# First product of the first layer in four of six token blocks, written as seven products of sums, with another opening

## The chip, the cores and the metric

The kernel runs on one core of one Trainium2 chip. The metric is device time in microseconds (us) for one launch: the median of the runs shown. TensorE is called PE here, its weight loads PEld, VectorE DVE, ScalarE ACT, GpSimd POOL, and SP is the engine whose queue issues nearly all DMAs.

## What is computed

A linear attention with decay (4 batches, 8 heads, 768 steps, head size 64) gives 3072 tokens of 512 values. Two layers follow, each with an input product to 2048 and an output product back to 512.

```
for t in range(S):
    state = gamma * state + k[t] (outer) v[t]
    y[t] = scale * q[t] @ state
x = y as (3072, 512)
h = x @ w_in;  x = maximum(0.01 * h, h) @ w_out        # first layer
h = x @ w2_in; out = (h * cos(h)) @ w2_out             # second layer
```

## The kernel before

**Numbers.** All data are float32. For a large product each operand is split into a rounded high part and the low rest, and `mm3` (L360 to L363) issues three matmuls: high by high, low by high, high by low. Weights arrive as int64 words, and are rounded in steps: two ACT operations (`exponent`), two on DVE (`fraction`, `top_bits`), an integer addition on POOL (`round_up`, L139), an ACT cast to the high part and a DVE subtraction for the low part. The 32 half tiles of the first layer's weights (16 slices `f`, parts 0 and 1) pass through this at the start; the second layer's weights later, in the same way, with results stored to HBM (`w2d`, `w2i`).

**Blocks.** Tokens go in six blocks of 512. The attention works in 24 units of 128 steps; an `excursion` is a unit's run of 64x64 matmuls, for unit u ("here") and for the scores of unit u+1 ("ahead") together. In the first layer a block needs, for each of 16 slices `f`, `gemm1` (12 matmuls 128x512 into PSUM bank `p`), the leaky ReLU on ACT, a split into high and low (`high_g` on ACT, `low_g` on DVE), and the second product (12 matmuls 128x512 into four banks `acc`), one to three slices later. Blocks 0 and 1 are cut at slices 7 and 4 (`SPLIT`) and alternate, since their weights are still being made; blocks 2 to 5 run whole, with the attention of the block ahead and the second layer's weights beside them.

**Second layer.** It handles two blocks at a time, and its input product already goes by 2x2x2 pieces: seven products of sums in place of eight (names P1 to P7), with the weights' sums in `w2i` (1.83 MB for two slices), loaded in four DMAs, and the tokens' sums in `xq`. Its matmuls are 128x512.

**Order.** Everything stands in an order written by hand: strings (`LOADS`, `FIRST`, `SLOTS`, `TICKS`) for the opening, lists of steps by half slices afterwards, and an `Agenda` of moments (two per slice) for the second layer's weights: a half slice takes three moments, a pair of slices nine. Each engine runs its instructions in that order, and a DMA on SP waits until the eighth DMA before it has landed.

Of the kernel before, what the change touches and what calls it, by code (L numbers as in the profile page):

```python
# [24 lines left out]
P = 128  # L25
# [8 lines left out]
SPLIT = (7, 4)  # L34
# [26 lines left out]
XMADE = ("P1", "P2", "P3", "P5", "P7", "P6", "P4")  # L61

# [17 lines left out]
def body(ctx: ExitStack, tc: tile.TileContext, att, w1, w2, tab, out):  # L80
# [57 lines left out]
    def round_up(raw, t):  # L138
        nc.gpsimd.tensor_tensor(out=t, in0=t, in1=raw[:, :, 0], op=ALU.add)  # L139
# [7 lines left out]
    class Weights:  # L147
# [26 lines left out]
        def pieces(self):  # L174
# [34 lines left out]
    xq = [[dpool.tile([P, 1024], F32, name=f"xq{s}_{i}") for i in range(14)] for s in range(1, NB // 2)]  # L209
# [87 lines left out]
    def xprep(agenda, m, s, xlow=None, step=13):  # L297
# [9 lines left out]
        for k in range(2):  # L307
            way = {}
            for i, name, keep in ((0, "P1", True), (1, "P2", True), (3, "P3", True), (0, "P5", False), (2, "P7", False), (3, "P6", False), (1, "P4", False)):
                j = 7 * k + XMADE.index(name)  # L310
                if s == 0:
                    way[name] = parts(place(i), partial(own_x, j), 0, xlow or nc.vector, keep, None)
                else:
                    way[name] = parts(place(i), xq[s - 1][j], 0, nc.vector, keep, ostage, False)
# [17 lines left out]
    def load_xq(s, j):  # L332
        assert ("x", s) in made
        xt[j] = w_tile(j, 0, F32R, 1024)
        nc.sync.dma_start(out=xt[j].bitcast(F32), in_=xq[s - 1][j])

    def own_x(j):
        if j not in xt:
            xt[j] = w_tile(j, 0, F32R, 1024)
# [9 lines left out]
    wi = {}  # L349

    def load_wi(p, place):
        assert ("p", p) in made
        for old in [o for o in wi if wi[o][1] == place]:
            del wi[old]
        t = xpool.tile([P, 4096], F32R, tag=f"b{place}", name=f"b{place}")
        wi[p] = t, place
        for lo, hi in ((0, 1024), (1024, 2048), (2048, 3072), (3072, WIN)):
            nc.sync.dma_start(out=t[:, lo:hi].bitcast(F32), in_=w2i[p][:, lo:hi])
# [7 lines left out]
    class Attention:  # L366
        def __init__(self, apool, tb):
            self.apool, self.tb = apool, tb
            self.spare = [w_tile(NF - 1 - i // 2, i % 2, F32, 1024) for i in range(2 * EARLY)]
# [3 lines left out]
        def part(self, d, u, part, tag, bufs):  # L373
            if u < EARLY:
                d[u] = self.spare[2 * (EARLY - 1 - u) + part]
# [23 lines left out]
        def excursion(self, now, nxt, banks):  # L399

            sc, kv, po = (b.rearrange("p (n i) -> p n i", n=H) for b in banks)
# [58 lines left out]
        def tokens(self, u, xh, xl, tok0):  # L460
            x = self.apool.tile([P, KD, C], F32, tag="xs", name="xs", bufs=2)
# [11 lines left out]

    def new_x(n):
# [5 lines left out]
    def gemm1(key, f, x, hp):  # L480
        w = wslot[key, f, 0]
        xh, xl = x
        for k in range(KD):
# [21 lines left out]
    with tc.manual_schedule():  # L505

        with ExitStack() as pctx, ExitStack() as actx:
            apool = actx.enter_context(tc.tile_pool(name="apool", bufs=1))
            tb = apool.tile([P, NTAB], F32, name="tb", bufs=1)
            heads = Attention(apool, tb)  # L510

            NU = B * NCH
            xs = {}

            def excursion(u, banks):
                heads.excursion(u if u >= 0 else None, u + 1 if u + 1 < NU else None, banks)

            def evacuate(u):
                n = u // CPB
                if n not in xs:  # L520
# [8 lines left out]
            def unit_steps(u):  # L529
                def both():  # L530
                    excursion(u, [bank(i) for i in (1, 2, 3)])
                    scored(u + 1)
                    evacuate(u)
                    heads.lower[u](nc.gpsimd)
# [11 lines left out]
                return [both, int, state, int, values, int, int, int]  # L546

            def block_steps(n):
                return [step for u in range(n * CPB, n * CPB + CPB) for step in unit_steps(u)]

            agenda = Agenda()
            START, LAST = 4, 2 * (NF * (NB - 3) - 4)
            m, turn = 0, 0
# [10 lines left out]
            def half(f):  # L567
# [4 lines left out]
                high, low = parts(t, w2d[f], 0, nc.gpsimd, False, ostage)  # L572
# [37 lines left out]
            OWN = 4  # L610
            for p in range(OWN):
                for f in range(4 * p, 4 * p + 4):
                    half(f)
                pair(p)
            xprep(agenda, max(m + 3, LAST + 5), 0, nc.gpsimd)
# [395 lines left out]
```

## Time and profile before

| | us |
|---|---|
| median of 3 runs | 1105.61 (1105.3 to 1107.13) |
| the profiled execution | 1106.15 |
| its span, first to last instruction | 1104.4 |
| PE busy | 1078.5 (98% of the span) |
| DVE busy | 650.2 (59%) |
| ACT busy | 488.4 (44%) |
| POOL busy | 225.1 (20%) |

A busy PE is not PE at its peak: matmuls are pipelined, and a record's length is not the distance to the next one. The distance between starts is what counts. The granted clock is given as a share of 2.4 GHz; 0.50 is the lower level of 1.2 GHz.

### The profile page before, as it was taken

What the parts mean: (1) busy time and instruction counts of PE and PEld (TensorE: products, weight loads), DVE (VectorE), ACT (ScalarE), POOL (GpSimd) and SP (SyncE); (2) the same over time, 40 slices, a digit from 0 to 9 for tenths busy, and PEclk for the clock granted to TensorE, in tenths of its full rate; (3) what the DMA queues carried; (4) which work ended last, traced back from release to release, by engine and by line L of the source; (5) the groups of instructions that cost most, each with busy time, mean ns of one, the idle gap of its engine ahead of it and who ended that gap; (6) DMA issues with size and microseconds to landing.
All of it is one profiled execution on the core that took longest, in us unless ns stands there. A gap on an engine that the chain in (4) does not pass through costs nothing.

```text
span 1104.4 us, 18719 instructions
## 1 busy us (share of the span) xinstructions
PE 1078.5 (98%) x7484; PEld 893.3 (81%) x7484; DVE 650.2 (59%) x973; ACT 488.4 (44%) x842; POOL 225.1 (20%) x174
## 2 busy tenths in 40 slices
PE   4899999999999999999999999999999999999998
PEld 4678888888887887888888888888888888888887
DVE  3687843122444434333587677777767777656665
ACT  3677632223434334333554455544445544444432
POOL 3454421112434343332465000000000000000000
PEclk8799999999999999999999999999999999999999
DMA  9455422233545535533696436676446585423412
GB/s 366 165 195 203 153 77 83 72 115 115 170 151 191 177 123 189 173 108 116 196 326 240 144 135 226 211 283 229 142 173 239 183 311 207 164 72 143 156 54 77
DMA packets 71367, 189.22 MB, mean 171 GB/s; under 512 B 8048, under 2 KB 10352, under 8 KB 71280
## 3 DMA queue, kind: packets, MB, share of 16 engines
q1 hardware_dynamic: 71136, 187.50, 49.1%
q8 instruction: 59, 0.97, 0.4%
q10 hardware_dynamic: 144, 0.52, 0.1%
q14 instruction: 28, 0.23, 0.1%
HBM read 135.57 MB, written 52.43 MB: 170 GB/s over the span
## 4 chain that ended last, share of the span: by engine, by line
PE 89%; DMA 4%; issue 3%; POOL 2%; ACT 1%; DVE 1%; SPq 0%; POOLq 0%; ACTq 0%; DVEq 0%
PE p L361 18%; PE p L363 18%; PE p L362 18%; PE acc L361 11%; PE acc L362 11%; PE acc L363 11%; PE p L405 2%; DMA cbuf<-w 2%; DMA w<-att 1%; PE p L408 1%; POOL cbuf L139 1%; DMA w2d<-o 0%; POOL b L470 0%; POOL cbuf L275 0%; PE acc L408 0%
## 5 line engine op out<-in xcount | busy, mean ns | idle before, releaser
L361 PE MATMUL p<-b,w 128*128 128x512 f32 x384 | 150.7, 392 | 3.1 <-ACT t L490 3.1
L361 PE MATMUL acc<-g,w 128*128 128x512 f32 x384 | 151.4, 394 | 0.9 <-DVE o L692 0.9
L362 PE MATMUL acc<-g,w 128*128 128x512 f32 x384 | 149.7, 390 | 0.8 <-DVE w L145 0.8
L362 PE MATMUL p<-b,w 128*128 128x512 f32 x384 | 149.7, 390 | 0.0
L363 PE MATMUL p<-b,w 128*128 128x512 f32 x384 | 149.6, 390 | 0.0
L363 PE MATMUL acc<-g,w 128*128 128x512 f32 x384 | 149.6, 390 | 0.0
L361 PE MATMUL p<-w,b 128*128 128x512 f32 x336 | 130.7, 389 | 0.0
L362 PE MATMUL p<-w,b 128*128 128x512 f32 x336 | 130.7, 389 | 0.0
L363 PE MATMUL p<-w,b 128*128 128x512 f32 x336 | 130.7, 389 | 0.0
L502 DVE TENSOR_TENSOR g<-t,g 128x512 fp32r<-128x512 f32 x96 | 91.0, 950 | 53.5 <-ACT g L498 53.5
L490 ACT ACTIVATE t<-p 128x512 f32<-128x512 f32 x96 | 57.2, 596 | 117.3 <-PE p L363 110.5
L361 PEld LDWEIGHTS p<-b,w 128*128 128x128 f32 x384 | 72.3, 188 | 20.4 <-ACT t L490 5.3
L361 PEld LDWEIGHTS acc<-g,w 128*128 128x128 f32 x384 | 72.1, 188 | 17.0 <-DVE o L692 1.3
L362 PEld LDWEIGHTS acc<-g,w 128*128 128x128 f32 x384 | 72.1, 188 | 15.6 <-DVE w L145 1.1
L363 PEld LDWEIGHTS p<-b,w 128*128 128x128 f32 x384 | 72.2, 188 | 15.2
L363 PEld LDWEIGHTS acc<-g,w 128*128 128x128 f32 x384 | 72.1, 188 | 15.1
L362 PEld LDWEIGHTS p<-b,w 128*128 128x128 f32 x384 | 72.2, 188 | 14.8
L498 ACT CAST g<-t 128x512 fp32r<-128x512 f32 x96 | 59.4, 619 | 52.2 <-PE acc L363 51.9
L830 ACT ACTIVATE k<-d,bias 128x512 int32<-128x512 f32 x24 | 17.4, 723 | 141.8 <-DVE d L817 141.8
L835 ACT ACTIVATE r<-r,bias 128x512 f32<-128x512 f32 x96 | 69.7, 726 | 18.7 <-DVE r L832 18.7
L362 PE MATMUL p<-w,w 128*128 128x512 f32 (+1 forms) x196 | 75.4, 385 | 0.0
L363 PE MATMUL p<-w,w 128*128 128x512 f32 (+1 forms) x196 | 75.4, 385 | 0.0
(124 smaller groups left out, 2091.5 us busy)
## 6 DMA issues: line engine op xcount, KB each, us to landing
b<-w2i SPq DMA_DIRECT2D x60, 512.0 KB, 5.8
w<-w SPq DMA_DIRECT2D x32, 512.0 KB, 8.5
w<-w2d SPq DMA_DIRECT2D x32, 512.0 KB, 8.2
w<-xq SPq DMA_DIRECT2D x28, 512.0 KB, 5.9
cbuf<-w SPq DMA_DIRECT2D x24, 512.0 KB, 4.1
xq<-o SPq DMA_DIRECT2D x40, 256.0 KB, 2.3
vs<-att SPq DMA_DIRECT2D x18, 512.0 KB, 3.9
kq<-att SPq DMA_DIRECT2D x18, 512.0 KB, 5.6
```

What stands on the lines that cost most here:

```text
L139: nc.gpsimd.tensor_tensor(out=t, in0=t, in1=raw[:, :, 0], op=ALU.add)
L361: nc.tensor.matmul(o, sh, mh, start=start, stop=False)
L362: nc.tensor.matmul(o, sl, mh, start=False, stop=False)
L363: nc.tensor.matmul(o, sh, ml, start=False, stop=stop)
L405: return lambda: nc.tensor.matmul(out, stationary, moving, start=True, stop=True)
L408: return lambda start, stop: nc.tensor.matmul(out, stationary, moving, start=start, stop=stop)
L490: nc.scalar.activation(out=t, in_=hp, func=AF.Prelu, alpha=0.01)
L498: nc.scalar.copy(out=pair[:, 0], in_=g)
L502: eng.tensor_tensor(out=pair[:, 1], in0=g, in1=pair[:, 0].bitcast(F32), op=ALU.subtract)
L830: nc.scalar.activation(out=k, in_=h, func=AF.Identity, bias=bias[:, 0:1], scale=1.0)
L835: nc.scalar.activation(out=r, in_=r, func=AF.Sin, bias=bias[:, 1:2], scale=TURN)
```

## The change

**Seven products in blocks 2 to 5.** The loop over slices ends after blocks 0 and 1. A new `first_layer(i)` handles a pair of slices: seven products of two `mm3` each, 42 matmuls of 128x256 (half a block's tokens), in place of two `gemm1` with 24 matmuls of 128x512. Two products share a PSUM bank. DVE puts the seven results together (one copy and seven additions of 128x256), ACT applies the slope, and the two second products of the pair run one pair later. `low_g` of one slice of the pair is on POOL.

**Sums.** `first_pair` makes the weight sums of eight pairs beside blocks 0 and 1 (on DVE, with one subtraction on POOL and four casts on ACT for each pair) and stores them to `w1i`; `load_wi` brings them back, 1.83 MB for a pair in four DMAs, into two places of four weight slots, issued two pairs ahead. Its order of pairs turns round in every second block, so six pairs are loaded per block. `x_steps` makes the tokens' sums of a block (seven casts, seven subtractions for low parts, four differences).

**Moments.** There are four for a pair as before, but the agenda starts 8 moments sooner, five pairs of the second layer's weights go through it instead of four, and three through the late rooms instead of four.

**Opening.** Keys and queries of unit 0 and the tables come in one DMA (`first`), all on SP; the loads stand in another order; the first product starts one unit of attention sooner; "here" and "ahead" may stand apart; `gemm1` uses banks 0 and 3 in turn (`hidden_at`); `SPLIT` is (5, 4); `round_up` of the first layer's weights moves from POOL to DVE.

```
-SPLIT = (7, 4)
+SPLIT = (5, 4)
+    def round_up(raw, t, eng=nc.gpsimd):
+        eng.tensor_tensor(out=t, in0=t, in1=raw[:, :, 0], op=ALU.add)
...
-                round_up(raw, t)
+                round_up(raw, t, nc.vector)
...
+        def load_first(self):
+            self.kq[0] = self.first[:, :1024]
+            nc.sync.dma_start(out=self.first, in_=first)
...
-            LOADS = "ktLsskLsTkskskL"
-            FIRST = "vwsvegkmwweGmxgvevGmgywexGyvxmyLwgGwLvexymwgeGwswwgmwwL"
+            LOADS = "ksksskLssL"
+            FIRST = "vamvgkweGmgxkvGwewwgwvwwxmayGwwmywgLvwhhxGLasxmyyvkgG"
...
+            def first_pair(p, b, way):
...
+                def whole():
+                    for i in range(2):
+                        sub2(held(i), w()[i][:, :512], w()[i][:, 512:], ALU.add)
...
+                agenda.put(b, plain, whole)
+                agenda.put(b + 1, lambda: pair_sums(held(0), held(1)))
+                agenda.put(b + 2, g2[0], g3[0])
+                agenda.put(b + 3, g2[1], g3[1], lambda: made.add(("a", p)))
...
-            for seg, (n, f0, f1) in enumerate(SEGMENTS):
+            for seg, (n, f0, f1) in enumerate(SEGMENTS[:4]):
...
-                    hp = bank(f % 4 if n == NB - 1 else 0)
+                    hp = bank(hidden_at(f - f0))
...
+            def first_layer(i):
...
+                    for k in range(2):
+                        h, l = w_part(key, name, k)
+                        mm3(o, h, l, x[:, k * HALF : k * HALF + HALF], x[:, 512 + k * HALF : 512 + k * HALF + HALF], k == 0, k == 1)
...
+                p1, p6 = product("P1"), product("P6")
+                nc.vector.tensor_copy(out=a, in_=p1)
+                add(b, p6, a)
+                p7, p5 = product("P7"), product("P5")
+                add(c, p7, b)
+                add(d, p5, c)
+                add(b, p5, b)
+                p2, p4 = product("P2"), product("P4")
+                add(a, p2, a)
+                add(c, p4, c)
+                slope(second)
+                add(b, product("P3"), b)
+                follow(i)
+                g = high_g(second)
+                slope(first)
+                moment(0)
+                fn, *args = pending.pop(0)
+                fn(*args)
+                ready(second, g, 2 * p + 1, 0)
+                moment(1)
+                moment(2)
+                while len(pending) > 1:
+                    fn, *args = pending.pop(0)
+                    fn(*args)
+                ready(first, high_g(first), 2 * p, 1)
+                moment(3)
```

**Order, the opening on SP.** `att` is a unit's keys and queries (before L382, after L433) or its values (before L386, after L437), `w` a half of the first layer's weights, `tab` the tables, `first` the new joint load; unit 0's values come by ACT's queue before. Before, from the first DMA:

```order
L382 DMA w_0_160<-att 128x1024
L648 DMA tb<-tab 128x76
L119 DMA w_0_164<-w 128x1024
L386 DMA w_1_159<-att 128x1024
L382 DMA w_0_158<-att 128x1024
L119 DMA w_0_170<-w 128x1024
L386 DMA w_1_157<-att 128x1024
L648 DMA tb<-tab 128x512
L382 DMA w_0_156<-att 128x1024
```

After, from the first DMA to the keys and queries of unit 3:

```order
L429 DMA first<-first 128x1612
L437 DMA w_0_182<-att 128x1024
L433 DMA w_1_181<-att 128x1024
L437 DMA w_0_180<-att 128x1024
L437 DMA w_0_178<-att 128x1024
L433 DMA w_1_179<-att 128x1024
L128 DMA w_0_190<-w 128x1024
L437 DMA w_0_176<-att 128x1024
L437 DMA w_0_174<-att 128x1024
L128 DMA w_0_194<-w 128x1024
L433 DMA w_1_177<-att 128x1024
```

Keys and queries of unit 2 move from the ninth place (the tenth transfer with ACT's) to the sixth; those of unit 3 are the eleventh.

**Order, a half tile of weights on DVE,** in the first slices of block 0; `cbuf` holds the words in work, `g` is `low_g`. Before:

```order
L395 TENSOR_TENSOR vp<-vs,tb 128x512
L129 TENSOR_SCALAR cbuf<-cbuf 128x512
L134 SCALAR_TENSOR_TENSOR cbuf<-w_0_663,cbuf 128x512
L145 TENSOR_TENSOR w_1_743<-cbuf,w_1_743 128x512
L502 TENSOR_TENSOR g<-t,g 128x512
```

After:

```order
L138 TENSOR_SCALAR cbuf<-cbuf 128x512
L143 SCALAR_TENSOR_TENSOR cbuf<-w_1_608,cbuf 128x512
L148 ISA cbuf<-w_1_608,cbuf 128x1024
L154 TENSOR_TENSOR w_0_805<-cbuf,w_0_805 128x512
L569 TENSOR_TENSOR g<-t,g 128x512
```

The addition of `round_up` is a fourth DVE operation for each half tile; it is listed as 1024 half words.

**Order, the loop of blocks 2 to 5, on DVE and on SP.** Before, DVE for two slices with an excursion between them (`sf`, `state`, `xs` are the attention's):

```order
L502 TENSOR_TENSOR g<-t,g 128x512
L441 TENSOR_TENSOR sf<-p_2981,tb 128x512
L454 TENSOR_TENSOR state<-p_2982,state 128x256
L462 TENSOR_TENSOR xs<-p_2983,tb 128x512
L502 TENSOR_TENSOR g<-t,g 128x512
L129 TENSOR_SCALAR cbuf<-cbuf 128x512
L134 SCALAR_TENSOR_TENSOR cbuf<-cbuf 128x512
L454 TENSOR_TENSOR state<-p_2982,state 128x256
```

After, DVE for a pair of slices without an excursion:

```order
L285 TENSOR_TENSOR cbuf<-cbuf,o 128x512
L1035 COPY t<-p_3095 128x256
L1026 TENSOR_TENSOR t<-p_3095,t 128x256
L1026 TENSOR_TENSOR t<-p_3110,t 128x256 x3
L1026 TENSOR_TENSOR t<-p_3126,t 128x256 x2
L1026 TENSOR_TENSOR t<-p_3142,t 128x256
L138 TENSOR_SCALAR cbuf<-cbuf 128x512
L143 SCALAR_TENSOR_TENSOR cbuf<-cbuf 128x512
L569 TENSOR_TENSOR g<-t,g 128x512
```

SP before, in block 3 (`cbuf<-w` fetches raw weights of the second layer, `w2d` takes them back):

```order
L386 DMA vs<-att 128x1024
L382 DMA kq<-att 128x1024
L237 DMA w2d_100<-cbuf 128x512
L247 DMA cbuf<-w 128x1024
L237 DMA w2d_101<-o 128x512
L237 DMA w2d_101<-cbuf 128x512
```

SP after, two pairs of block 2:

```order
L395 DMA w_0_3459<-w1i_122 128x1024
L395 DMA w_0_3461<-w1i_122 128x1024
L395 DMA w_0_3463<-w1i_122 128x1024
L395 DMA w_0_3465<-w1i_122 128x512
L247 DMA w2d_95<-o 128x512
L247 DMA w2d_95<-cbuf 128x512
L257 DMA cbuf<-w 128x1024
L247 DMA w2i_108<-o 128x512
L395 DMA w_0_3573<-w1i_123 128x1024
L395 DMA w_0_3575<-w1i_123 128x1024
```

The results' additions go in front of the rounding steps on DVE, and the loads of weight sums in front of fetches and stores on SP.

## Rows read from the trace of the kernel before

**Rows 1.** The page: span, then busy time, share and instructions of each engine.

```profile
span 1104.4 us, 18719 instructions
PE 1078.5 (98%) x7484; PEld 893.3 (81%) x7484; DVE 650.2 (59%) x973; ACT 488.4 (44%) x842; POOL 225.1 (20%) x174
```

**Rows 2.** Windows by stage: start:end, length, busy per engine (instructions), clock, DMA share, GB/s.

```profile
0.00:38.20 38.20, 20.28 (x689) 19.09 (x689) 16.30 (x29) 15.04 (x35) 15.45 (x20) 0.75 0.94 367
38.20:75.00 36.80, 34.65 (x441) 27.61 (x443) 29.63 (x46) 26.43 (x57) 15.16 (x12) 0.98 0.35 116
75.00:240.00 165.00, 165.00 (x1362) 136.70 (x1354) 82.58 (x122) 70.98 (x125) 48.38 (x37) 1.00 0.37 122
240.00:540.00 300.00, 297.33 (x2527) 245.02 (x2526) 121.49 (x175) 115.04 (x203) 104.31 (x79) 1.00 0.46 150
540.00:620.00 80.00, 80.00 (x355) 66.26 (x354) 61.57 (x70) 39.57 (x74) 41.84 (x27) 1.00 0.66 239
```

**Rows 3.** PE's weight loads for `gemm1`: line, engine, operation, count, busy us, mean ns.

```profile
L361 PEld LDWEIGHTS p<-b,w 128*128 128x128 f32 x384 | 72.3, 188 | 20.4 <-ACT t L490 5.3
```

**Rows 4.** PE's timeline, around one excursion and near the end: start, us, line, tiles, shape.

```profile
298.30 0.39 PE L363 MATMUL p<-b,w 128*128 128x512 f32 x1
...
300.64 0.50 PE L361 MATMUL acc<-g,w 128*128 128x512 f32 x1
...
1093.72 0.39 PE L362 MATMUL p<-w,w 128*128 128x512 f32 x1
...
1098.03 0.39 PE L363 MATMUL p<-w,w 128*128 128x512 f32 x1
1098.25 0.28 PE L361 MATMUL p<-w,w 128*128 128x256 f32 x1
...
1101.00 0.28 PE L363 MATMUL p<-w,w 128*128 128x256 f32 x1
```

**Rows 5.** The chain of waits in the opening: start, us, what.

```profile
6.11 10.02 DMA w<-att
...
20.34 2.60 issue
...
28.43 0.90 issue
...
34.77 0.83 issue
...
38.21 0.72 PE p L361
```

**Rows 6.** DVE and POOL groups by shape.

```profile
L134 DVE SCALAR_TENSOR_TENSOR cbuf<-w,cbuf 128x512 int32<-128x512 int32 x32 | 23.3, 730 | 1.1
L139 POOL TENSOR_TENSOR cbuf<-cbuf,w 128x512 int32<-128x512 int32 x32 | 48.0, 1499 | 65.7 <-DVE cbuf L134 51.4 <-ACT g L498 5.9 <-issue 5.4
L454 DVE TENSOR_TENSOR state<-p,state 128x256 f32<-128x256 f32 x35 | 14.7, 420 | 5.3 <-PE p L408 4.6 <-PE p L405 0.6
```

**Rows 7.** The chain in block 2: one fetch and rounding of second layer's weights.

```profile
329.76 4.25 DMA cbuf<-w
334.03 0.67 ACT cbuf L124
...
337.35 0.63 ACT o L268
```

**Rows 8.** Windows of 5 us with DMA near full (columns as in rows 2).

```profile
550.00:555.00 5.00, 5.00 (x23) 4.14 (x23) 4.97 (x6) 2.77 (x5) 2.71 (x3) 1.00 0.98 346
570.00:575.00 5.00, 5.00 (x24) 4.14 (x23) 3.37 (x6) 2.04 (x4) 2.86 (x3) 1.00 1.04 410
```

**Rows 9.** DMA issues: KB each, median us to landing; 0:25, 550:575, whole run.

```profile
w<-w SPq DMA_DIRECT2D x9, 512.0 KB, 10.2
...
raw<-w SPq DMA_DIRECT2D x3, 512.0 KB, 7.7
...
b<-w2i SPq DMA_DIRECT2D x60, 512.0 KB, 5.8
```

More of the change, by code (lines that the diff above doesn't have):

```diff
@@ L349, in body, with pair_of, follow, load_wi @@
     wi = {}
-    def load_wi(p, place):
-        assert ("p", p) in made
+    NQ = NF // 2
+    def pair_of(q):
+        return q % NQ if q // NQ % 2 == 0 else NQ - 1 - q % NQ
+    turns = [("a", pair_of(q)) for q in range(NQ * (NB - 2))] + [("p", pair_of(q)) for q in range(NQ * NB // 2)]
+    def follow(i):
+        if i + 2 < len(turns) and turns[i + 2] not in wi:
+            load_wi(turns[i + 2], wi[turns[i]][1])
+    def load_wi(key, place):
+        assert key in made
         for old in [o for o in wi if wi[o][1] == place]:
             del wi[old]
[L355 to L358, printed above, removed]
+        src = (w1i if key[0] == "a" else w2i)[key[1]]
+        tiles = []
+        for i, slot in enumerate(WSLOTS[place]):
+            n = min(1024, WIN - 1024 * i)
+            t = w_tile(slot, 0, F32R, 1024)
+            nc.sync.dma_start(out=t[:, :n].bitcast(F32), in_=src[:, 1024 * i : 1024 * i + n])
+            tiles.append(t)
+        wi[key] = tiles, place
+    def w_part(key, name, k):
+        hi, lo = WCOLS[name]
+        t = wi[key][0][hi // 1024]
+        return (t[:, at % 1024 + k * P : at % 1024 + k * P + P] for at in (hi, lo))
     def mm3(o, sh, sl, mh, ml, start, stop):
@@ L374, in part @@
             if u < EARLY:
-                d[u] = self.spare[2 * (EARLY - 1 - u) + part]
+                n = 2 * (EARLY - 1 - u) + 1 - part
+                d[u] = self.spare[n] if n < len(self.spare) else self.first[:, :1024]
             else:
@@ L399, in excursion @@
         def excursion(self, now, nxt, banks):
-            sc, kv, po = (b.rearrange("p (n i) -> p n i", n=H) for b in banks)
+            sc, kv, po = (b.rearrange("p (n i) -> p n i", n=H) if b is not None else None for b in banks)
             rows = [slice(r * D, r * D + D) for r in range(2)]
@@ L670, in ask @@
                     heads.prep_v(u, VBY[u])
-                elif c == "e":
-                    excursion(u - 1, [acc_bank(i) for i in range(3)] if u <= CPB and u % 2 == 0 else [bank(i) for i in (1, 2, 3)])
+                elif c in "eah":
+                    now = next(nu["H"]) if c in "eh" else None
+                    nxt = next(nu["A"]) if c in "ea" else None
+                    excursion(now, nxt)
                 elif c == "m":
@@ L787, in body @@
+            plan_closed = []
+            for i in range(NQ * (NB - 2)):
+                first_layer(i)
+                if 4 * i + 3 >= when[NU - 1] + 3 and not plan_closed:
+                    plan_closed.append(1)
                     actx.close()
@@ L963, in body @@
             spare()
-            if q + 2 < QUADS and pair_of(q + 2) not in wi:
-                load_wi(pair_of(q + 2), wi[pair_of(q)][1])
+            follow(NQ * (NB - 2) + q)
             if q > 0:
```

329 lines of the change are left out of this document (245 added, 84 removed).

## The prediction

> **What bounds the kernel now.** I read the totals first, then the windows by stage, then the chain of waits inside the stages that have gaps. PE is busy in 1078.5 of 1104.4 us, and no other engine passes 59% [rows 1]. By stage, PE idles 38.20 - 20.28 = 17.9 us in the opening, 2.2 us up to 75, nothing up to 240, 2.7 us from 240 to 540, nothing from 540 to 620 [rows 2]. So outside the opening the time is the number of matmuls times the distance between them. That distance comes from starts, not from the length of a record: (1098.03 - 1093.72) / 19 = 0.2268 us for 128x512, and (1101.00 - 1098.25) / 23 = 0.1196 us for 128x256 [rows 4]. An excursion of the attention takes 300.64 - 298.30 - 0.23 = 2.1 us [rows 4]. The chain in the opening runs through a late transfer of keys and queries (6.11 to 16.13), waits called issue, and DVE; the first large matmul starts at 38.21 [rows 5].
>
> The sum is made against the profiled execution: span 1104.4, with 1.75 us around it to its own 1106.15. The median, 1105.61, is the span plus 1.2, and I add 1.2 at the end.
>
> **1. Seven products: -13.4 us.** A pair of slices had 24 matmuls of 128x512 in its first product, 24 x 0.2268 = 5.44 us; it gets 42 of 128x256, 42 x 0.1196 = 5.02 us. Four blocks of eight pairs: 32 x 0.42 = 13.4 us. So an eighth less arithmetic gives only 7.7%, since the narrow matmul costs a little over half of the wide one. It all lies on PE, which has no idle time there to hide it. The 128x256 distance is taken from a stretch with nothing beside it; a weight load takes 0.188 us [rows 3], more than 0.1196, yet in that stretch the matmuls stayed 0.12 apart, so the loads overlap each other as well. Were they to bind in the loop, this term turns over (rival 4).
>
> The Trainium skill ("TensorE: Matmul & The Clock Gate", section "Back-to-back issue gap") gives an isolated gap of N/2.4 + 2.5 ns: 215.8 and 109.2 ns here. By it the term would be 768 x 0.2158 - 1344 x 0.1092 = 19.0 us (an estimate from that page). The trace has about 13 ns over N/2.4 at either width, not 2.5, and since the narrow form pays this overhead 1344 times instead of 768, the measured distances decide.
>
> What hides the rest of the new work: DVE needs eight operations of 128x256 per pair, 8 x 0.42 = 3.4 us by the nearest form, an addition from PSUM at 420 ns [rows 6]. They run as the products finish; only the last three follow P3. After the products PE has second products of the pair before (24 x 0.2268 = 5.44 us), longer than additions and slope, and the next pair starts in other banks. Without that cover up to 3.4 us would show per pair, 109 us in all; I take 0, because the product of one pair and the use of its result are a whole pair apart. DVE's total in blocks 2 to 4, 121.5 of 300 us before [rows 2], gains 24 x 3.4 = 82 us and the tokens' sums, and stays under 80%.
>
> **2. The opening: -8.6 us.** Before, keys and queries of unit 2 are the tenth transfer, behind 4.5 MB; at 367 GB/s [rows 2] that would be 12.3 us, and they landed at 16.1 [rows 5], 3.9 late. After, unit 3's are the eleventh, behind 6.07 MB: 16.5 + 3.9 = 20.4 us. The first product now stands one unit earlier; a unit takes 34.77 - 28.43 = 6.3 us of the chain [rows 5]. 20.4 + 6.3 gives a first large matmul near 27 (25 if the transfer is not late, 33 if a whole unit is lost again), instead of 38.2: -11.2. One excursion moves behind it, +2.1; two banks for `gemm1` take away short gaps, -1.5 of the 2.2 us up to 75 [rows 2]; the weights of the first slices now have less time, +2 (0 to 5, the latter half the 10.2 us that a weight load took there [rows 9]). Together -8.6; bounds -13 to -3.
>
> **3. Gaps in blocks 2 to 4: -2.7 us.** They are half slices that waited for ACT and DVE; 24 matmuls in a row now stand in front of each. Between 0 and -2.7; I take all of it, since new gaps are costed apart.
>
> **4. `round_up` on DVE: +1 us.** It has no row on DVE. Below: an operation of 128x512 on int32, 0.73 [rows 6]; above: POOL's 1.50 for the same work [rows 6]. I take 0.8, the row of the same engine and type. Queued behind it on DVE are `low_g`, which the next second product waits for, and the masks of the attention. From 38 to 75 us DVE was busy 29.6 of 36.8 us [rows 2], with nine of these half tiles in it: 9 x 0.8 = 7.2 fills it to 36.8. So DVE has no room in that stretch, while POOL's 65.7 us of waits before L139 [rows 6] leave the path. The two cover each other nearly; +1, bounds 0 to 11 (rival 3). The sums for `w1i` come beside blocks 0 and 1, where DVE has half its time from 75 to 240 [rows 2]: nothing.
>
> **5. Loads: +3 us.** Each pair of blocks 2 to 5 loads 1.835 MB, 26 times in all after those made in place. Where the DMA is fullest, from 540 to 620, it moved 239 GB/s x 80 us = 19.1 MB [rows 2]; block 5 gets six more loads, 11.0 MB, so 30.1 MB in eight pairs of 10.47 us (5.02 + 5.44), 83.8 us. At 410 GB/s, reached at 570 [rows 8], that is 73 us and fits; at 346, at 550 [rows 8], it is 87, and 3 us are missing. The first five pairs hold 25.4 MB, 62 us at 410 against 52.3: 9.6 us behind, covered by about 10 us (a load is issued a pair and a half, 15.7 us, ahead of its use and needs 5.8 when the queue is free [rows 9]). Blocks 2 to 4 have at most 4.7 MB in 10.9 us, under 410. Between 0 and 15 (five pairs at 346: 73 against 52, less the ten, and 4 for SP's order); I take 3.
>
> By the Trainium skill ("DMA: Bandwidth & Descriptors", section "Specifications") HBM gives about 358 GB/s to a core. Then block 5's 30.1 MB would need 84.1 us of its 83.8 (an estimate from that page). This trace shows 367 over 38 us and 410 in a window of 5 [rows 2, 8], so the row decides, but it holds for short stretches only.
>
> **6. Waits called issue ahead of the attention: +2 us.** In the opening, with a full DMA, they took 2.60 + 0.90 + 0.83 = 4.33 us [rows 5] over five excursions; at a DMA share of 0.46 PE lost 2.7 us in all over twelve. Sixteen excursions remain for the loop with more loads: 0 to 16 x 0.87 = 14; its DMA share stands nearer the second row, so +2.
>
> **Sum.** 1104.4 - 13.4 - 8.6 - 2.7 + 1 + 3 + 2 = 1085.7, and 1.2 more: **1087**.
>
> **Rivals.**
> *1. The opening starts no earlier.* Unit 3's keys and weights queue up, and the first large matmul stays near 36: the term of part 2 goes from -8.6 to -2.2 + 2.1 - 1.5 + 2 = 0.4, 1096 (1093 to 1103). For it: 3.9 us of lateness already, and 6 MB ahead instead of 4.5. Against: the DMA is full at 0.94 either way, and work that doesn't depend on unit 3 starts sooner.
>
> *2. The chain of fetches falls behind (slower).* Second-layer weights are fetched into few buffers, and the next fetch waits until a half is rounded: 4.25 us of fetch and 3.3 beyond it, 337.35 - 329.76 = 7.6 [rows 7]. After, 26 of them must go through 93 moments of blocks 2 to 4; 24 pairs of 10.47 and some twelve excursions of 2.1 make 2.87 us a moment, 93 x 2.87 / 26 = 10.3 us each. So a fetch may take 7.0 us; each us more costs 26 us, of which some 8 are slack, and the gains are gone at 8.0. Where the DMA was full a fetch of this size took 7.7 (550 to 575) and 10.2 (opening) [rows 9], so it is possible: at 8.5, 39 - 8 = 31 more, 1118 (1108 to 1135). Against: the share from 240 to 540 was 0.46 and stays under 1 in most pairs.
>
> *3. DVE becomes the bound in blocks 0 and 1.* If an integer addition costs twice a plain one, 1.4 us, the 19 or so of 32 half tiles that meet a full DVE pay 0.58 over the 0.8 each: 11 us, 1098 (1096 to 1105).
>
> *4. The change doesn't do what it says:* weight loads keep matmuls of 128x256 at 0.188 us: 1344 x (0.188 - 0.1196) = 92 more, 1179.
>
> **How the numbers follow.** The forecast has 0.55 (1079 to 1094), all gains without costs and an opening at 25 has 0.04 (1077), rival 1 has 0.15, rival 2 0.14, rival 3 0.10, rival 4 0.02. A measurement of this kernel can tell about 0.2%, 2.2 us, from no change. Faster holds the forecast, the best case, rival 1 and most of rival 3: 0.55 + 0.04 + 0.15 + 0.08 = 0.82. Same: 0.02 of rival 3 and 0.03 of rival 2, 0.05. Slower: 0.11 and 0.02, 0.13. The range from 1077 to 1104 leaves out rivals 2 and 4 and little else.
>
> **What would show it.** The first large matmul near 27; starts of 128x256 matmuls 0.12 apart in blocks 2 to 5, with no PE idle before the second products; L148 near 0.8 us; the latency of `cbuf<-w` fetches under 7 us; a DMA share under 1 in most of block 5. Wrong would be: large PE idle time in blocks 2 to 5 released by DMA (part 5, rival 2) or by DVE additions (part 1), a first large matmul at 33 or later (part 2), or PE waiting for `low_g` or weights before 150 us (part 4).

## The result and the profile after

| | us |
|---|---|
| before, median of 4 (1105.3 to 1107.13) | 1105.69 |
| after, median of 4 (1117.89 to 1126.36) | 1121.88 |
| ratio after to before, 95% interval | 1.0146 (1.0119 to 1.0173) |
| the profiled execution of after | 1126.36 |
| its span | 1124.6 |

The changed kernel is 16 us slower; the forecast was 1087. Its four executions also lie further apart (8.5 us) than the four of before (1.8), and the profiled one is the longest of them, 4.5 us over the median.

The page's totals of after, to hold against [rows 1]: span, then busy time, share and instructions of each engine.

```profile
span 1124.6 us, 20622 instructions
PE 1083.3 (96%) x8060; PEld 923.2 (82%) x8060; DVE 792.3 (70%) x1373; ACT 500.8 (45%) x854; POOL 169.3 (15%) x140
```

PE is busy for longer than before, although its work should have shrunk by 13.4 us. The windows by stage (start:end, length, busy per engine with instructions, granted clock, DMA share, GB/s; [rows 2] has those of before) show why:

```profile
0.00:75.00 75.00, 57.73 (x1172) 50.70 (x1173) 53.14 (x89) 36.54 (x74) 15.47 (x22) 0.95 0.71 263
75.00:240.00 165.00, 164.30 (x1316) 135.94 (x1315) 131.91 (x221) 80.53 (x144) 24.16 (x19) 1.00 0.68 231
240.00:540.00 300.00, 288.44 (x2938) 258.56 (x2936) 198.78 (x401) 122.08 (x213) 112.19 (x88) 0.98 0.76 261
540.00:636.00 96.00, 87.89 (x494) 76.76 (x493) 66.02 (x124) 37.14 (x67) 17.44 (x12) 0.95 0.94 353
```

From 240 to 636 us, blocks 2 to 5, PE is idle for 11.6 + 8.1 = 19.7 us (before: 2.7), and its clock, which was 1.00 there before, is 0.98 and 0.95: time in which PE is busy but slow. The DMA moves 261 GB/s in place of 150, then 353.

Busy time hides both, so I counted PE's lost time: the length of a stretch less what its matmuls need at the distances of [rows 4] (0.2268 us for 128x512, 0.12 for 128x256) and 2.0 us for an excursion's 132 small ones; with the 2.1 of [rows 4] both rows would be lower by the same amount. The last column ends at 612 us before and 632 after, some 492.5 us ahead of either end; the second layer's first products already stand in it.

| lost by PE, us | 0 to 75 | 75 to 240 | 240 to 540 | 540 to 612 or 632 |
|---|---|---|---|---|
| before | 32.5 | 1.9 | 8.3 | 0 |
| after | 32.6 | 3.5 | 25.3 | 14.1 |

The opening gave nothing, and the loop of blocks 2 to 5 loses 31 us more than before (39.4 against 8.3). 31 and 1.7 (the two stretches up to 240 us) less 13.4 (fewer and narrower matmuls) is 19; the spans differ by 20.2.

What PE waited for in the loop, by the view of waits of PE (us in total, times, longest): first before, from 240 to 617 us, then the four largest of after, from 240 to 640 us.

```profile
PE p L361 <- ACT t L490: 1.8, 3, 0.9
PE acc L361 <- DVE o L692: 0.9, 1, 0.9
```

```profile
PE p L459 <- DVE t L1026: 7.3, 5, 2.8
PE p L405 <- DVE t L1026: 4.2, 2, 2.7
PE acc L405 <- ACT o L837: 3.2, 2, 1.9
PE acc L407 <- DVE g L569: 2.9, 1, 2.9
```

None of them names a DMA. But in most of these waits DVE, ACT and POOL were not busy either; one has to follow a wait back. Here is the one of 2.8 us, in order of time, from the timelines of SP, ACT, POOL, DVE and PE (in brackets: idle time of the engine before, and what ended it):

```profile
490.11 0.33 SPq L257 DMA_DIRECT2D cbuf<-w  x1
492.86 2.71 SPq L395 DMA_DIRECT2D w<-w1i  x4
495.46 0.67 ACT L133 ACTIVATE cbuf<-cbuf 128x512 f32<-128x512 f32 x1 [4.73 <-DMA cbuf<-w]
496.16 0.43 DVE L138 TENSOR_SCALAR cbuf<-cbuf 128x512 int32<-128x512 int32 x1 [7.25 <-ACT cbuf L133]
496.59 0.60 ACT L565 CAST g<-t 128x512 fp32r<-128x512 f32 x1
497.27 1.26 POOL L569 TENSOR_TENSOR g<-t,g 128x512 fp32r<-128x512 f32 x1 [5.17 <-ACT g L565]
498.56 1.55 DVE L1026 TENSOR_TENSOR t<-p,t 128x256 f32<-128x256 f32 x4 [0.46 <-POOL g L569]
499.84 1.05 PE L459 MATMUL p<-sf,vp 64*64 64x64 f32 x18 [2.82 <-DVE t L1026]
```

A fetch of the second layer's words lands 5.3 us after its issue. ACT has stood at that rounding step (L133) for 4.7 us. Two ways lead from there to the additions. DVE stands 7.25 us at its own rounding step (L138), which needs ACT's result and has the additions behind it in DVE's order. And `high_g` (L565) is behind L133 in ACT's order, `low_g` on POOL behind that, and the additions need the tile `t` that `low_g` reads, which holds DVE 0.46 us longer. PE needs the bank that the additions empty. At a block's end a store does the same: DVE stands 5.7 us until `w2d<-o` has landed and `o` is free, ACT 6.9 us at a fetch, and the evacuation of the accumulators (L837, L839) comes late.

```profile
341.04 0.66 ACT L133 ACTIVATE cbuf<-cbuf 128x512 f32<-128x512 f32 x1 [6.93 <-DMA cbuf<-w]
341.79 0.69 DVE L839 TENSOR_SCALAR o<-acc 128x512 f32<-128x512 f32 x1 [5.72 <-DMA w2d<-o]
342.78 0.56 PE L405 MATMUL acc<-g,w 128*128 128x512 f32 x1 [1.87 <-ACT o L837]
343.14 0.63 PE L406 MATMUL acc<-g,w 128*128 128x512 f32 x1
343.56 0.63 PE L407 MATMUL acc<-g,w 128*128 128x512 f32 x1
```

Right behind that wait the matmuls stand 0.42 us apart, not 0.23: by the windows the granted clock is 0.50, the lower of the two levels, from 343.07 to 346.48.

```profile
343.07:346.48 3.41, 3.41 (x9) 2.65 (x9) 2.51 (x7) 0.65 (x2) 2.53 (x2) 0.50 0.83 308
```

Nine matmuls there cost some 1.8 us more. The clock falls five times in blocks 2 to 5 of this execution, for 3.4 us four times and 6.8 us once, 20.5 us in all, each time during or after a wait of PE; at half speed that is up to 10 us. With 19.7 us of idle time this makes up the loop's loss.

### The profile page after: what moved, and what is told of

It reads as the page before. It is cut to its first block, busy times and chain, and to the rows that moved or that the text cites. A ratio compares the mean times of both kernels' runs of the same rounds, so it can differ in the third digit from the quotient of the medians.

```text
span 1124.6 us, 20622 instructions
## 1 busy us (share of the span) xinstructions
PE 1083.3 (96%) x8060; PEld 923.2 (82%) x8060; DVE 792.3 (70%) x1373; ACT 500.8 (45%) x854; POOL 169.3 (15%) x140
## 4 chain that ended last, share of the span: by engine, by line
PE 48%; DVE 3%; issue 3%; DMA 2%; POOL 2%; ACT 1%; SPq 0%; POOLq 0%; DVEq 0%; ACTq 0%
PE p L405 11%; PE p L407 11%; PE p L406 11%; PE acc L407 5%; PE acc L406 5%; PE acc L405 5%; DVE t L1026 1%; DMA cbuf<-w 1%; POOL cbuf L148 1%; DMA w2i<-o 1%; POOL g L569 1%; DMA raw<-w 0%; ACT t L1029 0%; POOL o L285 0%; DVE cbuf L295 0%
## 5 line engine op out<-in xcount | busy, mean ns | idle before, releaser
L405 PE MATMUL p<-b,w 128*128 128x512 f32 (+1 forms) x572 | 196.8, 344 | 4.6 <-DVE t L1026 4.2
L406 PE MATMUL p<-b,w 128*128 128x512 f32 (+1 forms) x572 | 196.1, 343 | 0.0
L407 PE MATMUL p<-b,w 128*128 128x512 f32 (+1 forms) x572 | 196.1, 343 | 0.0
L405 PE MATMUL p<-w,w 128*128 128x512 f32 (+1 forms) x532 | 185.8, 349 | 0.0
L406 PE MATMUL p<-w,w 128*128 128x512 f32 (+1 forms) x532 | 185.7, 349 | 0.0
L407 PE MATMUL p<-w,w 128*128 128x512 f32 (+1 forms) x532 | 185.7, 349 | 0.0
L405 PE MATMUL acc<-g,w 128*128 128x512 f32 x384 | 154.5, 402 | 4.8 <-ACT o L837 3.2
L407 PE MATMUL acc<-g,w 128*128 128x512 f32 x384 | 151.8, 395 | 2.9 <-DVE g L569 2.9
L406 PE MATMUL acc<-g,w 128*128 128x512 f32 x384 | 152.0, 396 | 0.2 <-DVE w L154 0.2
L405 PEld LDWEIGHTS p<-b,w 128*128 128x128 f32 x572 | 108.9, 190 | 19.7 <-DVE t L1026 5.0
L406 PEld LDWEIGHTS p<-b,w 128*128 128x128 f32 x572 | 109.0, 191 | 13.7 <-DVE w L154 0.4
L407 PEld LDWEIGHTS p<-b,w 128*128 128x128 f32 x572 | 109.0, 190 | 12.3
L405 PEld LDWEIGHTS p<-w,w 128*128 128x128 f32 x532 | 100.8, 190 | 13.0
L406 PEld LDWEIGHTS p<-w,w 128*128 128x128 f32 x532 | 100.7, 189 | 13.0
L407 PEld LDWEIGHTS p<-w,w 128*128 128x128 f32 x532 | 100.7, 189 | 12.9
L1026 DVE TENSOR_TENSOR t<-p,t 128x256 f32<-128x256 f32 x224 | 84.0, 419 | 25.6 <-POOL g L569 18.6
L405 PEld LDWEIGHTS acc<-g,w 128*128 128x128 f32 x384 | 73.7, 192 | 21.7 <-ACT o L837 3.9
L407 PEld LDWEIGHTS acc<-g,w 128*128 128x128 f32 x384 | 73.4, 191 | 19.3 <-DVE g L569 3.3
L406 PEld LDWEIGHTS acc<-g,w 128*128 128x128 f32 x384 | 73.5, 191 | 14.2 <-DVE w L154 0.5
L1029 ACT ACTIVATE t<-t 128x512 f32<-128x512 f32 x64 | 40.3, 629 | 96.0 <-DVE t L1026 96.0
L1108 ACT ACTIVATE r<-r,bias 128x512 f32<-128x512 f32 x96 | 69.6, 725 | 18.6 <-DVE r L1105 18.6
```

What stands on the lines that cost most here:

```text
L405: nc.tensor.matmul(o, sh, mh, start=start, stop=False)
L406: nc.tensor.matmul(o, sl, mh, start=False, stop=False)
L407: nc.tensor.matmul(o, sh, ml, start=False, stop=stop)
L1026: nc.vector.tensor_tensor(out=out, in0=o, in1=s, op=ALU.add)
L1029: nc.scalar.activation(out=t, in_=t, func=AF.Prelu, alpha=0.01)
L1108: nc.scalar.activation(out=r, in_=r, func=AF.Sin, bias=bias[:, 1:2], scale=TURN)
```

## The experiments

Medians; the ratio to the runs of before on the same chip stands with its interval. "The loads" are those of the first layer's weight sums, `w<-w1i`.

### Are the loads the cause, and by what?

```
-            load_wi(turns[i + 2], wi[turns[i]][1])
+            key, (tiles, place) = turns[i + 2], wi[turns[i]]
+            if key[0] == "p":
+                load_wi(key, place)
+                return
...
+            wi[key] = tiles, place
```

> Left out: the loads of the first layer's weight sums in blocks 2 to 5 after the first two (the tiles keep the first two pairs' sums, so the output is another); everything else is as in the changed kernel. Theory A (the 1.83 MB loads lengthen the fetches of the second layer's weights; ACT and DVE wait for these at the head of their queues, and low_g, the additions and so PE behind them): the loop's lost time falls to about that of before, 1092 to 1102 us against 1122. Theory B (the eight operations on DVE and the order of work on DVE, ACT and POOL cost the time whatever the DMA does): 1115 or more.

1091.44 us, 0.9867 (0.9852 to 0.9882). All 30 us go, and theory B falls: the additions, the order of work and the opening are unchanged. PE is never idle in the loop (windows of this run):

```profile
240.00:540.00 300.00, 300.00 (x3061) 270.96 (x3060) 217.16 (x438) 135.79 (x239) 117.94 (x91) 1.00 0.53 173
540.00:606.00 66.00, 66.00 (x384) 58.60 (x384) 48.50 (x92) 26.47 (x47) 11.43 (x8) 1.00 0.79 267
```

The DMA issues from 240 to 540 us show what the loads do to the others (KB each, median us to landing), first with the loads (after), then without, last in the kernel before:

```profile
cbuf<-w SPq DMA_DIRECT2D x25, 512.0 KB, 4.9
vs<-att SPq DMA_DIRECT2D x9, 512.0 KB, 6.8
w2d<-o SPq DMA_DIRECT2D x16, 256.0 KB, 7.4
```

```profile
cbuf<-w SPq DMA_DIRECT2D x25, 512.0 KB, 4.2
vs<-att SPq DMA_DIRECT2D x9, 512.0 KB, 5.8
w2d<-o SPq DMA_DIRECT2D x16, 256.0 KB, 4.2
```

```profile
cbuf<-w SPq DMA_DIRECT2D x24, 512.0 KB, 4.1
w2d<-o SPq DMA_DIRECT2D x16, 256.0 KB, 4.3
```

Single fetches (`cbuf<-w`) take 3.5 to 5.7 us in before and 3.8 to 8.0 in after.

Bytes or the place in SP's order: the same four DMAs into the tiles that are there, with an eighth of the columns.

```
+            for j, t in enumerate(tiles):
+                n = min(1024, WIN - 1024 * j) // 8
+                nc.sync.dma_start(out=t[:, :n].bitcast(F32), in_=w1i[key[1]][:, 1024 * j : 1024 * j + n])
```

> As the first run, but the four DMAs of each load are issued with an eighth of their columns: the same instructions on SP, an eighth of the bytes (the rest of the sums is old, so the output is another). Theory A by bytes: within 4 us of the first run. Theory A by order on SP (a fetch stands behind four more DMAs and their waits for earlier ones, whatever their size): 1112 or more.

1092.11 us, 0.9871 (0.9856 to 0.9886): the bytes. Then half of them (`// 2`), which leaves the low parts of the sums old:

> As a2_small_loads with half the bytes of each load (0.92 MB, so the output is another). If the cost is in proportion to the bytes: half of 30 us, 1104 to 1109. If it begins only where the DMA is nearly full (share 0.53 without loads, 0.76 with them, from 240 to 540 us): 1093 to 1100.

1097.26 us, 0.9921 (0.9907 to 0.9934). Half the bytes cost 6 us, the other half 25. From 240 to 540 us the DMA share is 0.53 without loads, 0.68 with half and 0.76 with all (windows of this run, the stretch from 240 to 540 us):

```profile
240.00:540.00 300.00, 296.69 (x3025) 267.00 (x3024) 211.96 (x432) 131.88 (x231) 115.91 (x90) 1.00 0.68 224
```

The cost is not in proportion to the bytes. That the share itself sets it doesn't follow: runs below have as high a share and lose less.

Where the 30 us are, with the loads left out of blocks 2 to 4 alone (`if key[0] == "p" or i + 2 >= 24`):

> Left out: the loads of the first layer's weight sums for blocks 2 to 4 (20 of 26; the tiles keep old sums, so the output is another); the six of block 5 stay. It divides the 30 us that the loads cost. By PE's gaps in the trace after, about half of it lies past 540 us, where the second layer's loads and stores run too: 1104 to 1108 us. If block 5 has the cover that the prediction gave it (term 5: 3 us there): 1092 to 1096.

1104.77 us, 0.9991 (0.9982 to 1.0001). Block 5's six loads cost 13 us, the twenty of blocks 2 to 4 17. The seven products give back 13.4 / 4 = 3.4 us per block; the loads cost 17 / 3 = 5.7 on average in blocks 2 to 4 and 13 in block 5.

### Which transfers carry the cost

```
-                return lambda: fetch2(raw2(), f, part)
+                return lambda: None
```

> Left out: the 26 fetches of the second layer's raw weights into the one raw buffer in blocks 2 to 4 (old words are rounded, so the output is another); the loads of the sums stay. Theory A: the wait at the head of ACT's queue goes with the fetch, 1095 to 1108 us. If PE is held up by the loads of sums themselves, or by stores, or by DVE: 1114 or more.

1112.06 us, 1.0059 (1.0044 to 1.0074): between the two expectations. With the fetches 10 us of the 30 go; so do 13.6 MB of transfers (26 of 512 KB), so this run alone doesn't tell waiting from bytes.

Then stores that send from a tile that stays, so that no working buffer waits for a landing:

```
+        return wslot["a", 0, 1][:, :n].bitcast(F32)
...
-                send(dst[:, lo : lo + n], o[0], wait)
+                send(dst[:, lo : lo + n], kept(dst, o[0], n), wait)
...
-                send(dst[:, lo + n : lo + 2 * n], w, wait)
+                send(dst[:, lo + n : lo + 2 * n], kept(dst, w, n), wait)
```

> The stores of the second layer's weights send as many bytes as before, but from a tile that stays in place (other values, so the output is another): the working buffers o, cbuf and those of the late pairs are free when their steps are done, not when their store has landed, and SP needn't wait for the steps. Theory A, second half (the 20 us of the loads' cost that a3_no_fetch left are waits for buffers whose store lands late): 1098 to 1108 us. If those 20 us are sums that come late, or the lower clock by itself: 1115 or more.

1119.88 us, 1.0131 (1.0104 to 1.0158): alone hardly anything, against my expectation. And both:

> The run before without the 26 fetches as in a3_no_fetch; the loads of sums all stay. If short transfers at the head of ACT's and DVE's order carry the whole cost of the loads: 1090 to 1098 us, as without the loads. If the loads themselves hold up PE: 1104 or more.

1105.16 us, 0.9995 (0.9985 to 1.0004). I had put the limit of the other theory at 1104, so by the total this misses. By stage it is plain (windows of this run):

```profile
240.00:540.00 300.00, 299.61 (x3057) 270.36 (x3056) 219.75 (x436) 129.83 (x230) 118.17 (x90) 1.00 0.73 240
540.00:636.00 96.00, 87.44 (x457) 74.58 (x456) 63.19 (x115) 39.48 (x69) 12.42 (x9) 0.95 0.86 321
```

In blocks 2 to 4 PE is idle for 0.4 us although all loads are there: they do not hold up PE themselves, the waits for the fetches and for the stores' buffers do. Taking away one of the two gave 10 or 2 us, both together 17. Nor is it the bytes that went with the fetches: the DMA still moved 240 GB/s, more than in e4_half_loads (224), where PE was idle for 3.3 us. And the stores land as late as in after; only nobody waits for them (240 to 640 us of this run):

```profile
w2d<-w SPq DMA_DIRECT2D x32, 256.0 KB, 7.7
```

Block 5 keeps its whole loss, 13.7 us over a1_no_loads. Of what waits there these runs leave in place the raw words of the late pairs and the tokens' sums. In a7 as in after ACT stood 10.3 us at one of the latter, for an `o` whose store `xq<-o` was late; here is the row of a7:

```profile
581.74 0.62 ACT L283 CAST o<-t 128x512 fp32r<-128x512 f32 x1 [10.34 <-DMA xq<-o]
```

In after that stop ends at 601.1 us, and PE's wait of 2.9 us at 603.7 is for `low_g` behind it. PE's two other long waits of block 5, 1.5 us at 559 and 2.7 at 571, are of another kind: DVE itself has no room there.

```profile
550.00:573.00 23.00, 19.91 (x121) 17.30 (x119) 22.36 (x38) 10.67 (x20) 6.41 (x4) 1.00 1.02 391
```

DVE is busy in 22.36 of these 23 us, and the additions stand behind a heap of rounding steps. That the heap comes from steps that waited for transfers earlier is not shown; without the loads DVE is nearly as full (20.40 of the 23 us from 540 to 563 in a1_no_loads), and PE never waits. So the loads cost the 13 us of block 5, but by which way was not separated.

### Other places for the same work

The loads one by one, behind the moments of a pair, not four in a row ahead of them:

```
-                follow(i)
+                parts_left = follow(i) or []
...
+                    if parts_left:
+                        parts_left.pop(0)()
```

> The four DMAs of a load one by one, each behind one of the pair's four moments, in place of four in a row ahead of them: the same bytes, and at most 0.5 MB stands ahead of a fetch or a store. Theory A1 (what is lost is the latency of short transfers behind 1.83 MB in a row): 1102 to 1112 us. Theory A2 (the DMA is simply full, bytes per block decide): 1116 to 1124.

1114.90 us, 1.0084 (1.0065 to 1.0103), 7 us better: worse than theory A1, better than A2. From 240 to 540 us PE is idle 7.3 us in place of 11.6, but in block 5 the sums now come late themselves. The waits of PE from 540 us on, in that run:

```profile
PE p L422 <- DMA w<-w1i: 10.8, 7, 2.9
```

`high_g` and `low_g` ahead of the rounding steps:

```
                 ready(second, g, 2 * p + 1, 0)
+                ready(first, high_g(first), 2 * p, 1)
                 moment(1)
                 moment(2)
-                while len(pending) > 1:
+                while len(pending) > 2:
...
-                ready(first, high_g(first), 2 * p, 1)
                 moment(3)
```

> high_g and low_g of the pair's other slice stand ahead of the second and third moment's rounding steps on ACT and POOL, in place of behind them. If PE's waits for additions come from low_g that stands behind a waiting rounding step (t is not free for the additions): 1108 to 1116 us. If the waits come from elsewhere (stores' buffers, sums that are late), or if ACT now waits for a free g instead: 1118 to 1126.

1128.70 us, 1.0203 (1.0188 to 1.0218): worse. DVE's 18.6 us of waits for `low_g` are gone, but DVE's own rounding step now waits 38.0 us for ACT's (31.5 in after, 240 to 640 us), ACT stands 54.0 us at fetches (48.5) and PE up to 4.0 us at the evacuation of a block. Both together give the sum of the two differences (7 us less, 7 us more):

> Both of the runs before together. If they take away different parts of the loss: 1096 to 1106 us, at or below the kernel before; if they are two views of one wait: as the better of them.

1121.96 us, 1.0147 (1.0128 to 1.0166). And more time for a fetch, with `exponent` one moment later:

```
-                for i, step in zip((0, 2, 3, 3, 4, 5), (begin
+                for i, step in zip((0, 3, 3, 3, 4, 5), (begin
...
-                times = (0, 2, 3, 3, 3, 5, 6, 6, 4, 5, 7, 8, 8, 9, 9, 10, 10)
+                times = (0, 3, 3, 3, 3, 6, 6, 6, 4, 5, 7, 8, 8, 9, 9, 10, 10)
```

> The first rounding step (exponent, on ACT) of each second-layer half of blocks 2 to 4 stands one moment later, three moments behind its fetch in place of two, so a fetch may take some 8.6 us in place of 5.7 before ACT waits for it. If the fetch's latency against its place in ACT's order is what costs the 10 us that went with the fetches in a3_no_fetch: 1112 to 1117 us. If the steps that now stand close together on ACT, DVE and POOL make DVE wait in its place: 1120 to 1126.

1129.12 us, 1.021 (1.0194 to 1.0225): worse. ACT's waits for fetches halve (48.5 to 24.2 us), but DVE's for ACT's `exponent` grow from 31.5 to 39.7 us and those of ACT for POOL's `round_up` from 31.5 to 44.0: the step is now too near its followers. In this run and in b2_early_low moving a step that waits, or one behind it, passed the wait on.

Loads spread as in b1_spread, in blocks 2 to 4 alone (`if i + 2 < 24`), and 2 MB taken out of block 5 (the four loads left over are issued in the second layer):

```
+                    if f >= 12:
+                        agenda.soon(partial(load_wo, NF - 1 - f, f), 2)
+                    else:
+                        deferred.append(partial(load_wo, NF - 1 - f, f))
```

> Loads of sums one per moment in blocks 2 to 4 alone (in block 5 four in a row again, since there they came late in b1_spread), and four of block 5's eight loads of the second layer's output weights (2 MB) put behind the start of the second layer, which uses them later. Blocks 2 to 4 give 7 us as in b1_spread; block 5's 30 MB become 28, 5 us at 400 GB/s: 1108 to 1113 us. If block 5's loss hangs on single late transfers and not on its bytes: 1114 to 1117.

1109.91 us, 1.004 (1.0026 to 1.0054), as expected, 12 us better than the change, and the best whole version found; still 4 us behind the kernel before. What each of the two edits gave was not separated. Its windows:

```profile
240.00:540.00 300.00, 293.60 (x3002) 263.20 (x3001) 203.50 (x417) 127.28 (x223) 113.05 (x88) 1.00 0.80 273
540.00:636.00 96.00, 89.79 (x496) 76.85 (x495) 68.51 (x128) 41.30 (x73) 16.48 (x11) 1.00 0.95 348
```

PE is idle for 12.6 us in place of 19.7, at a higher DMA share than in after (0.80 against 0.76 from 240 to 540 us), and its clock stays at 1.00 from 240 to 636 us, where after had 20.5 us at 0.50. So between these two profiles up to 10 us of the gain are the clock.

With the later `exponent` on top:

> The run before with the later exponent of b3_later. If the fetches' latency and the loads in a row are two separate costs: 1103 to 1109 us; if spreading the loads has cured the fetches already: 1108 to 1114.

1124.32 us, 1.0183 (1.0162 to 1.0204): the later `exponent` costs 14 us here, 7 in b3_later.

### The opening

```
-                round_up(raw, t, nc.vector)
+                round_up(raw, t, nc.gpsimd)
```

> round_up of the first layer's weights back on POOL, all else as in the changed kernel. If the 0.69 us that it takes on DVE holds up the opening (values of the attention and low_g queue behind it there, the excursion at 48.6 us waits 2.2 us): 1116 to 1120, 2 to 6 us less. Rival: POOL's 1.5 us makes the weights late in its place, 1122 to 1128.

1125.19 us, 1.0173 (1.0156 to 1.019): `round_up` on POOL is no better in the changed kernel. It is 3 us worse by the medians, but the two intervals overlap (after: 1.0119 to 1.0173). The same step moved in the kernel before:

> The kernel before with one part of the change: round_up of the first layer's weights on DVE. By a4_round_pool (3 us slower with it on POOL in the changed kernel): 1102 to 1105 us. By term 4 of the prediction: 1106 to 1107 (+1); if DVE were full there as in rival 3: 1112 or more.

1105.21 us, 0.9999 (0.9989 to 1.0008): nothing. Two edits of the opening were tried without the loads, where little scatters. `VBY` (`1122010211` to `1122010111`) puts unit 7's values on POOL:

> On a1_no_loads (loads of sums left out, 1091.4 us, little scatter): the scaled values of unit 7 are made on POOL, which has no work there, in place of DVE, where they stand behind two half tiles of weights. PE's wait of 2.2 us at 48.9 goes if that queue is its cause: 1088 to 1090 us. If the wait is for the transfer of unit 7's values: 1091 to 1092.

1093.02 us, 0.9883 (0.987 to 0.9897). PE's wait grew from 2.2 to 3.5 us. The values now stand on POOL behind the growth of a state (L513), which waits for DVE, as this run's POOL timeline shows; so the queue on DVE holds both ways, and my edit had not gone round it.

```profile
50.36 0.61 POOL L513 TENSOR_TENSOR state<-state,first 128x256 f32<-128x256 f32 x1 [9.98 <-DVE state L511]
50.93 1.23 POOL L452 TENSOR_TENSOR vp<-vs,first 128x512 f32<-128x512 f32 x1
```

Unit 3's keys ahead of the first weights (`LOADS` from `ksksskLssL` to `ksksskkLssL`, one `k` less in `FIRST`):

> On a1_no_loads: keys and queries of unit 3 are the seventh transfer of SP in place of the eleventh, ahead of two halves of weights, so they land near 12 us in place of 20.4. If this transfer sets the opening, as the prediction's term 2 has it, the first large matmul starts some 8 us sooner and the time falls by 5 us or more: 1083 to 1087. If the chain of units (excursion, mask, growth, tokens) sets it, only the 1.9 us wait goes and the weights come later: 1089 to 1093.

1092.24 us, 0.9877 (0.9862 to 0.9892). The keys landed at 13.0 in place of 20.3 us, and the first large matmul stayed at 31.99 (32.14 without the edit). The transfer does not set the opening: the matmuls on the masks (`acc<-sf,vp`) started at 24.1 us with the edit, after a wait for DVE's `sf`, and at 24.2 without. The chain of units is what is left, though no run shortened it. With the edit the granted clock was also 0.50 from 22.42 to 29.25 us, without it 1.00 from 24.48; that may hide a gain of the 2 us of PE's wait for keys, not of the 8 us that I expected. Last, all of this in the best version:

> c2_spread24_defer (1109.9 us) with the two edits of the opening above and six in place of four of the output weights' loads put behind the start of the second layer. Two us for POOL, up to two for unit 3's keys, 2.5 for 1 MB less in block 5: 1102 to 1106, level with the kernel before or just below. If the opening's edits bring nothing: 1107 to 1110.

1111.25 us, 1.0045 (1.0031 to 1.0058): no gain over c2_spread24_defer, neither from the opening's edits nor from another 1 MB out of block 5.

## Why the prediction was wrong, point by point

**Term 1, the products: right.** In the loop of after 128x256 matmuls start 0.12 us apart, with weight loads of 0.19 us beside them:

```profile
281.22 0.28 PE L405 MATMUL p<-w,w 128*128 128x256 f32 x1
...
283.26 0.28 PE L407 MATMUL p<-w,w 128*128 128x256 f32 x1
```

(283.26 - 281.22) / 17 = 0.120. Rival 4 falls. By the formula in the section "Back-to-back issue gap" of the Trainium skill's page "TensorE: Matmul & The Clock Gate" the distance would be 0.109 (an estimate from that page); the trace keeps its 0.120. The eight operations are hidden, as term 1 said, when nothing else is late: a1_no_loads has no idle PE in the loop, with DVE busy 217 of 300 us there.

**Term 2, the opening: wrong**, by 8.6 us. The keys landed at 20.35 us, as worked out, but the first large matmul started at 31.94, not 27: I took one unit period behind the transfer, and e2_nl_kq3 shows that with keys 7 us sooner the first large matmul does not move. More important, an earlier first matmul is not time won. By 75 us PE has started 120 large and 1007 small matmuls before, 116 and 1056 after, which is the same work (0.9 us less, 0.7 more). What was won by 38.2 us (14 large matmuls for 1) was lost by 75, in waits of 2.2 us at 48.8 and 1.2 us at 59.0 among others. That is the price of rival 1 (0.4 in place of -8.6), by another reason than the one I gave it: the first large matmul did come sooner.

**Term 3, the gaps of blocks 2 to 4: right in a1_no_loads**, where they are gone; in after others take their place.

**Term 4, `round_up`: near right.** On DVE it takes 0.77 us (0.8 taken). In the kernel before its move is worth 0, from -1.2 to +0.9 us by the interval, so +1 lies just at the edge; in the changed kernel a4_round_pool, by its median, even makes it a gain of 3. Rival 3 falls.

```profile
L148 DVE CUSTOM_DVE_ANT_0 cbuf<-w,cbuf 128x1024 uint16<-128x1024 uint16 x32 | 24.6, 768 | 1.4
```

**Term 5, the loads: the step that failed.** I priced them at +3 with an upper bound of 15; they cost 30 (a1_no_loads). I asked only whether the bytes fit and whether the loads themselves come in time. They do come in time: by its waits, PE never waits for `w<-w1i` in after. I didn't ask what 1.83 MB in front of them does to short transfers on whose landing other engines stand in order. The median fetch went from 4.1 to 4.9 us and the store `w2d<-o` from 4.3 to 7.4, and a7_stores_free_no_fetch shows that waits for these two kinds carry all of blocks 2 to 4 (17 us); the way of the 13 us of block 5 stays open.

The term's own figures were not sound either. 4.7 MB in 10.9 us is 431 GB/s, over the 410 that it was said to stay under; and the 25.4 MB of block 5's first five pairs stand on no row: before moved 306 GB/s from 540 to 592 us, 15.9 MB, which with the six loads makes 27. But whether the bytes fit was not what decided: e4_half_loads lost 6 us at means of 224 (240 to 540 us) and 293 GB/s (540 to 636), far under 346 and 410.

The Trainium skill ("DMA: Bandwidth & Descriptors", section "Specifications") has 358 GB/s as HBM's share of a core. The trace of after moved 391 over the 23 us from 550 to 573, so that figure does not bound it.

**Term 6** was put down to attention and is part of term 5: PE's waits at excursions are for L1026, the additions.

**The two together.** 1087, 27 more for term 5 and 8.6 for term 2 make 1122.6; measured were 1121.88. Without the loads it would be 1087 - 3 + 8.6 = 1092.6; a1_no_loads took 1091.44.

**Rival 2** had the sign, the place and the range (1108 to 1135), with a chance of 0.14, but not the mechanism: fetches had to take 7 us before it cost anything. In after their median is 4.9, and 4 of 25 took over 7 (up to 8.0); they cost all the same, since a single late one stops ACT there and then (the one of 5.3 us above). Slack in the mean of a chain covers nothing where the waiting step stands first in an engine's order. And five times 3.4 to 6.8 us at the lower clock went with PE's stops, which no term had.

## What to carry to other kernels

Where transfers are added, ask first which short transfers will queue behind them, and who stands in order waiting for those; here half the bytes of the loads cost 6 us and the other half 25. The mean DMA share doesn't give the price: from 240 to 540 us 0.76 went with 11.6 us of idle PE (after), 0.80 with 6.4 (c2_spread24_defer), and 0.73 with 0.4 where nobody waited for the short transfers (a7_stores_free_no_fetch). Price a scheme with fewer matmuls by block: gain per block against bytes per block (here 3.4 us against 11 MB in a block with six loads). An earlier first matmul counts only if by the end of the opening more work is done.

## What the runs showed of the hardware beside that

- In after the granted clock fell from 1.00 to 0.50 in an otherwise full loop behind single waits of PE of 1.9, 2.8 and 2.7 us and behind two of 0.7 and 1.4 us close together, 0.2 to 1.1 us after their end, and once within a wait of 2.9 us; no fall came behind waits of 1.3 us at 443 and 1.5 us at 559. The same wait of the opening, 2.2 us at 49, was followed by 3.4 us at 0.50 in a1_no_loads (from 51.8) and by none in after. In before the clock never fell between 40 us and the end.
- Weight loads of 0.19 us each do not hold back matmuls of 0.12 us: in a1_no_loads neighbouring 128x256 matmuls of the loop start at most 0.121 us apart, over 1312 distances.
- Executions of the same kernel lie 8.5 us apart in after and 2.5 in a1_no_loads, four of each, and 2.5 over 19 of before. The loads alone don't explain it: a4_round_pool, b2_early_low and b3_later have them all, and their four lie 2.2 to 3.0 apart.
- Some DVE instructions took longer while POOL was busy. In after L295 on 128x512 took 0.68 to 0.69 us in 34 cases with POOL idle (or busy for under a fifth of it) and 1.1 to 1.8 in the six others; L1026, which reads a PSUM bank, kept 0.42 in either case (145 and 79). In block 5, on POOL and DVE:

```profile
556.18 1.69 POOL L148 TENSOR_TENSOR t<-t,raw 128x512 int32<-128x512 int32 x1 [0.63 <-DVE t L143]
556.63 1.79 DVE L295 TENSOR_TENSOR cbuf<-cbuf 128x512 f32<-128x512 f32 x1
561.47 0.68 DVE L295 TENSOR_TENSOR cbuf<-cbuf 128x512 f32<-128x512 f32 x1
```
